# Permuting the stages of an attention step: scores and exponential ahead of transposes and product

## The chip, the cores and the metric

The kernel runs on one core of a Trainium2 chip. The metric is device time in microseconds (us). The kernel before takes 703.48 us (median of 3 runs, 703.40 to 703.51). A core has five engines that matter here, each with a queue that it works off in the order in which the program put the instructions in: TensorE (PE; its weight loads are shown apart as PEld), VectorE (DVE), ScalarE (ACT), GpSimd (POOL) and SyncE (SP, which here issues nearly all DMAs).

## The reference

The first half is an attention in which a query sees only the keys of its own hash bucket; the second is a mixture of four experts, applied to the attention's output.

```python
# q, k, v: (2, 8, 768, 64); proj: (64, 6); batch 2, 8 heads, 768 rows
q_bucket = sum of 2**n * ((q @ proj)[n] > 0);  k_bucket likewise
scores = q @ k.T / 8, and -1e9 where q_bucket != k_bucket
attn = exp(scores - rowmax);  attn /= rowsum + 1e-9
x = (attn @ v), heads side by side: (1536, 512)
p = domain_probs / (rowsum + 1e-9)                 # (1536, 4)
out = sum over e of p[:, e] * (relu(x @ w1[e]) @ w2[e])   # w1 (4, 512, 1024)
```

## The kernel before

The attention goes head by head, 16 heads (`b`, `h`), and each head has six row tiles of 128 rows (`t`). One *step* `i` belongs to tile `i` of all 96. The work of a tile is cut into stages, and stage X of a step handles the tile some steps back (its lag), so that one step holds pieces of several tiles:

- **S** (lines 442 to 463, tile i): four matmuls, two by two, write 128 x 768 negated scores into a PSUM tile `sps` (two of these exist). VectorE copies them to the SBUF tile `p` and takes the row minimum `nb` on the way (line 454).
- **E** (line 470, tile i-1): ScalarE makes the exponential in place, with the row sum as a by-product.
- **T** (lines 502 to 521, tile i-3, the heads of batch 0 only): twice three TensorE transposes into PSUM tiles `ptps` (tag "one", of which there are four, shared with the product `pv` and the hash `hps`). Each triple is copied to SBUF (`pt` or `pth`): the first by ScalarE, the second by VectorE, or by ScalarE too in every third tile (steps 1 and 4 of a head).
- **X** and **Y** (lines 526 to 552, batch 1 only) do the same without TensorE: VectorE transposes 32 x 32 blocks, and two DMAs through DRAM do the rest.
- **V** (lines 554 to 572): the product with `v`, for a whole head. In batch 0 in two halves: the first in step 3 of the next head, one step after the last tile of its own head was transposed, the second in step 5. **U** (lines 577 to 592, step 2 of the head after that) copies the result out, one half by ScalarE, one by VectorE.
- **N**, **R** (lines 475 to 498): reciprocals of the row sums, sent through DRAM and back as a broadcast. **M** (line 594): POOL multiplies by them and splits the result in a high and a low part, every second head.
- **P**: preparation of the next head in four pieces, one per step 0 to 3: high half of q and k on ScalarE (line 376, step 1) and copies of it on POOL (line 265), low half on VectorE (line 379, step 2), hash matmuls (line 391) with the signs of their results on ScalarE (line 401, step 3), then the key columns on POOL (lines 406, 265). P also issues the next loads.

The order of the stages within a step is the string `ORDER`; the program is emitted by hand in this order, and each engine keeps it. For batch 0 the steps run alone, with the first expert's weights split on VectorE and POOL in between. From step 53 on, when the last head of batch 0 has been multiplied out, the MoE starts. Its first half runs over batch 0, and between its groups of matmuls the attention steps of batch 1 are drawn in: S, T and P give back a cost at a `yield`, and as many are drawn as the costs allow. From about 330 us on the MoE is alone.

Of the kernel before, what the change touches and what calls it, by code (L numbers as in the profile page):

```python
# [42 lines left out]
W_SPLIT = 40  # L43
W_STEP = 6
PREP_AT = 0
ORDER = "TXSUVMEYNRP"
LIGHT_FROM = 8
DRAIN = 2000
SPLIT_FIRST = 3
# [7 lines left out]
def tile_lsh_attention__then__domain_moe(  # L57
# [570 lines left out]
    def attention():  # L628
# [76 lines left out]
        for i in range(n + LAG_M[1] + 3):  # L705
            for op in ORDER:
                c = do(op, i)
# [509 lines left out]
```

## Time and profile before

| | |
|---|---|
| Median of 3 runs | 703.48 us |
| The profiled execution | 703.57 us |
| its span, first to last instruction | 701.9 us |
| Busy: TensorE / weight loads | 695.0 / 589.4 us |
| Busy: VectorE / ScalarE / POOL | 515.3 / 330.9 / 307.5 us |
| Granted TensorE clock, mean | 0.999 |

Busy times are sums of instructions. Matmuls overlap each other, so a TensorE that counts as busy may still be waiting; idle time of TensorE is better seen at its weight loads, each of which precedes its matmul. In a timeline a number in brackets is how long the engine was idle before the instruction, and behind the arrow stands what ended last of the things that it waited for; "issue" means that nothing was waited for that the profile shows. In the lists below one line can stand for several equal instructions in a row (x2, x3, x6).

### The profile page before, as it was taken

Reading aid. Unit: us, or ns where it says so; the run is one execution under the profiler, and the core shown is the slowest. Engines: PE = TensorE matmul, PEld = TensorE weight load, DVE = VectorE, ACT = ScalarE, POOL = GpSimd, SP = SyncE. Lnnn points to the kernel's source line nnn. Section 1 sums busy time; section 2 is a strip of 40 time slices with the busy share of each in tenths; the row PEclk is TensorE's granted clock in tenths of the full one; section 3 lists DMA queues with packets and bytes.
Section 4 is the critical chain, followed back from the end, with each engine's and each line's share of the span. In section 5 each row is a group of like instructions: output and inputs, shape, how many; then the busy total and the mean of one; then the engine's idle time right before and its main releaser. Section 6 shows DMA issues by size and latency. Waiting matters only on the chain.

```text
span 701.9 us, 10122 instructions
## 1 busy us (share of the span) xinstructions
PE 695.0 (99%) x3702; PEld 589.4 (84%) x3702; DVE 515.3 (73%) x839; ACT 330.9 (47%) x646; POOL 307.5 (44%) x290
## 2 busy tenths in 40 slices
PE   8999999999999999999999999999999999999998
PEld 7766675878878878877998989899898989989896
DVE  6898898967678568785768786777767667776762
ACT  7887788544543553551424444343333424343330
POOL 6359578623443543461525555342423324232420
PEclk9999999999999999999999999999999999999999
DMA  5323444669979778684221222411123121112202
GB/s 140 67 49 75 88 105 80 233 168 295 253 224 306 219 249 296 215 289 140 60 77 52 83 70 81 149 62 62 62 87 90 50 71 61 61 60 91 81 11 90
DMA packets 83938, 87.77 MB, mean 125 GB/s; under 512 B 52400, under 2 KB 54960, under 8 KB 81840
## 3 DMA queue, kind: packets, MB, share of 16 engines
q1 hardware_dynamic: 82864, 86.79, 41.4%
q8 instruction: 29, 0.48, 0.3%
q10 hardware_dynamic: 1024, 0.33, 0.2%
q14 instruction: 21, 0.17, 0.1%
HBM read 65.04 MB, written 22.07 MB: 124 GB/s over the span
## 4 chain that ended last, share of the span: by engine, by line
PE 94%; DVE 2%; POOL 2%; issue 1%; ACT 1%; DMA 0%; POOLq 0%; DVEq 0%
PE mps L786 13%; PE mps L788 12%; PE mps L787 12%; PE mps L1070 8%; PE mps L1074 8%; PE mps L1073 8%; PE pv L565 8%; PE sps L447 4%; PE sps L449 4%; PE ptps L515 4%; PE mps L836 3%; PE mps L838 3%; PE mps L837 3%; PE hps L391 1%; DVE p L454 1%
## 5 line engine op out<-in xcount | busy, mean ns | idle before, releaser
L786 PE MATMUL mps<-w2hi,hh 128*128 128x512 f32 (+1 forms) x388 | 150.6, 388 | 0.0
L788 PE MATMUL mps<-w2hi,hl 128*128 128x512 f32 (+1 forms) x388 | 150.3, 387 | 0.0
L787 PE MATMUL mps<-w2lo,hh 128*128 128x512 f32 (+1 forms) x388 | 150.3, 387 | 0.0
L1056 POOL TENSOR_TENSOR w2lo<-ws,w2hi 128x512 fp32r<-128x512 f32 x48 | 61.2, 1298 | 148.4 <-ACT w2hi L1055 146.9
L454 DVE TENSOR_SCALAR_CACHE_REDUCE p<-sps 128x768 f32<-128x768 f32 x96 | 90.3, 941 | 27.8 <-PE sps L449 26.1
L470 ACT ACTIVATE p<-p,nb 128x768 f32<-128x768 f32 x96 | 89.5, 932 | 24.1 <-DVE p L454 23.7
L780 DVE SCALAR_TENSOR_TENSOR acc<-mps,pe,acc 128x512 f32<-128x512 f32 (+1 forms) x85 | 63.0, 741 | 45.6 <-PE mps L788 45.2
L1074 PE MATMUL mps<-xo,w1lo 128*128 128x384 f32 x272 | 91.4, 336 | 0.0
L1073 PE MATMUL mps<-xo,w1hi 128*128 128x384 f32 x272 | 91.3, 336 | 0.0
L1070 PE MATMUL mps<-xo,w1hi 128*128 128x384 f32 x272 | 91.3, 336 | 0.0
L1080 ACT ACTIVATE hh<-mps 128x384 fp32r<-128x384 f32 x96 | 47.3, 492 | 92.5 <-PE mps L1074 62.9
L788 PEld LDWEIGHTS mps<-w2hi,hl 128*128 128x128 f32 x388 | 72.9, 188 | 15.2
L786 PEld LDWEIGHTS mps<-w2hi,hh 128*128 128x128 f32 x388 | 72.9, 188 | 14.5 <-issue 0.6
L787 PEld LDWEIGHTS mps<-w2lo,hh 128*128 128x128 f32 x388 | 72.9, 188 | 14.0
L1100 DVE TENSOR_TENSOR mt<-mps,mt 128x384 f32<-128x384 f32 x72 | 40.2, 558 | 45.2 <-PE mps L1074 44.4
L1014 POOL TENSOR_TENSOR w1lo<-ws,w1hi 128x512 fp32r<-128x512 f32 x36 | 49.5, 1378 | 44.3 <-ACT w1hi L1010 17.1
L565 PE MATMUL pv<-pt,tv 128*64 128x384 f32 x288 | 67.1, 492 | 0.0
L1085 DVE SCALAR_TENSOR_TENSOR hl<-mps,hh 128x384 fp32r<-128x384 f32 x96 | 53.4, 556 | 14.7 <-ACT hh L1080 12.4
L1010 ACT ACTIVATE w1hi<-wc 128x512 fp32r<-128x512 f32 x48 | 30.0, 630 | 66.6 <-DVE wc L1019 66.6
L265 POOL TENSOR_SCALAR q<-ah 64x768 fp32r<-64x768 f32 (+1 forms) x33 | 27.1, 822 | 76.2 <-ACT ah L376 61.9
L447 PE MATMUL sps<-ah,q 128*128 128x384 f32 x192 | 54.0, 362 | 0.4 <-DVE p L454 0.4
L534 DVE STREAM_TRANSPOSE t<-p 128x768 f32<-128x768 f32 x48 | 46.2, 964 | 8.5 <-ACT p L470 8.3
(137 smaller groups left out, 1372.2 us busy)
## 6 DMA issues: line engine op xcount, KB each, us to landing
ws<-in_moe_w_dram SPq DMA_DIRECT2D x64, 512.0 KB, 3.8
scr<-t SPq DMA_DIRECT2D x16, 1152.0 KB, 8.0
pt<-scr SPq DMA_DIRECT2D x16, 1152.0 KB, 6.8
tv<-in_v_dram SPq DMA_DIRECT2D x16, 192.0 KB, 5.9
tqk<-in_q_dram SPq DMA_DIRECT2D x30, 96.0 KB, 3.6
out_dram<-acc SPq DMA_DIRECT2D x11, 256.0 KB, 2.0
tqk<-in_k_dram SPq DMA_DIRECT2D x28, 96.0 KB, 3.7
rdb<-row SPq DMA_DIRECT2D x14, 192.0 KB, 4.5
```

What stands on the lines that cost most here:

```text
L447: nc.tensor.matmul(ps[:, i, :NH], q1[:, sl], k1[:, i * NH : (i + 1) * NH], start=True, stop=False)
L454: nc.vector.tensor_scalar(out=two(pt), in0=ps[:, :, :NH], scalar1=MASKED, scalar2=MASKED, op0=ALU.min, op1=ALU.min, accum_out=nb,)
L470: nc.scalar.activation(pt, pt, ACTF.Exp, bias=nb, scale=-1.0, accum_out=dens[b, h, r][:, o : o + 1])
L565: nc.tensor.matmul(dst, vvs[b, h][:, c], pts[b, h, g][c], start=c == 0, stop=c == NT - 1, tile_position=(0, g * D),)
L780: nc.vector.scalar_tensor_tensor(out=acc, in0=ps, scalar=pcol, in1=acc, op0=ALU.mult, op1=ALU.add)
L786: nc.tensor.matmul(ps, hh[:, ts], w2hi[:, f, cs], start=n == 0, stop=False)
L787: nc.tensor.matmul(ps, hh[:, ts], w2lo[:, f, cs], start=False, stop=False)
L788: nc.tensor.matmul(ps, hl[:, ts], w2hi[:, f, cs], start=False, stop=n == FC - 1)
L1056: nc.gpsimd.tensor_tensor(out=lo[:, c + o], in0=t[:, o], in1=hi[:, c + o].bitcast(F32), op=ALU.subtract)
L1070: nc.tensor.matmul(ps, whi[:, kk, fs], xh[kk], start=first and kk == 0, stop=False, skip_group_check=True)
L1073: nc.tensor.matmul(ps, whi[:, kk, fs], xl[kk], start=False, stop=False, skip_group_check=True)
L1074: nc.tensor.matmul(ps, wlo[:, kk, fs], xh[kk], start=False, stop=kk == KH - 1, skip_group_check=True)
```

## The change

The string that gives the order of the stages within a step is permuted: S ahead of T, and E directly behind S. U, V, M, Y, N, R and P keep their places to each other, and so do X and S. Lags, tiles and buffers stay.

```diff
-ORDER = "TXSUVMEYNRP"
+ORDER = "XSETUVMYNRP"
```

## Rows read from the trace of the kernel before

**Rows 1.** The page: the span, and the chain that ended last by engine.

```profile
span 701.9 us, 10122 instructions
...
PE 94%; DVE 2%; POOL 2%; issue 1%; ACT 1%; DMA 0%; POOLq 0%; DVEq 0%
```

**Rows 2.** Waits of weight loads, 125 to 702 us: total us, times, longest.

```profile
PEld sps L447 <- PE pv L565: 3.1, 5, 0.6
```

**Rows 3.** Timeline of weight loads, one head: start us, us, operation [idle <-releaser].

```profile
31.19 0.64 PEld L515 LDWEIGHTS ptps<-ident,p 128*128 128x128 f32 x6 [0.60 <-ACT p L470]
...
33.15 0.30 PEld L447 LDWEIGHTS sps<-ah,q 128*128 128x128 f32 x2
...
33.79 0.76 PEld L515 LDWEIGHTS ptps<-ident,p 128*128 128x128 f32 x6
...
35.15 0.42 PEld L515 LDWEIGHTS ptps<-ident,p 128*128 128x128 f32 x3
35.73 0.31 PEld L515 LDWEIGHTS ptps<-ident,p 128*128 128x128 f32 x3 [0.16 <-DVE pth L519]
...
36.91 0.13 PEld L565 LDWEIGHTS pv<-pt,tv 128*64 128x64 f32 x1 [0.24 <-issue]
...
38.58 0.13 PEld L391 LDWEIGHTS hps<-xt,pf 128*44 128x44 f32 x2 [0.18 <-issue]
...
39.64 0.64 PEld L515 LDWEIGHTS ptps<-ident,p 128*128 128x128 f32 x6 [0.61 <-issue]
...
41.04 0.31 PEld L515 LDWEIGHTS ptps<-ident,p 128*128 128x128 f32 x3
41.55 0.31 PEld L515 LDWEIGHTS ptps<-ident,p 128*128 128x128 f32 x3 [0.21 <-ACT pt L521]
...
42.73 0.13 PEld L565 LDWEIGHTS pv<-pt,tv 128*64 128x64 f32 x1 [0.24 <-issue]
...
44.82 0.64 PEld L515 LDWEIGHTS ptps<-ident,p 128*128 128x128 f32 x6 [0.60 <-ACT p L470]
```

**Rows 4.** Timeline of ScalarE in the same head.

```profile
31.77 0.49 ACT L521 ACTIVATE pth<-ptps 128x384 f32<-128x384 f32 x1 [1.17 <-PE ptps L515]
...
33.12 0.87 ACT L521 ACTIVATE pth<-ptps 128x384 f32<-128x384 f32 x2
33.88 0.94 ACT L470 ACTIVATE p<-p,nb 128x768 f32<-128x768 f32 x1
...
34.80 0.93 ACT L376 ACTIVATE ah<-xt,qk_scale 128x768 fp32r<-128x768 f32 x1
35.63 0.48 ACT L521 ACTIVATE pth<-ptps 128x384 f32<-128x384 f32 x1
36.00 0.48 ACT L592 ACTIVATE xr<-pv 64x384 f32<-64x384 f32 x1
...
39.82 1.17 ACT L401 ACTIVATE k<-hps,sgn_bias 44x384 fp32r<-44x384 f32 x2 [1.13 <-PE hps L391]
41.01 0.87 ACT L521 ACTIVATE pt<-ptps 128x384 f32<-128x384 f32 x2
```

**Rows 5.** Timeline of VectorE in the same head.

```profile
34.24 0.96 DVE L454 TENSOR_SCALAR_CACHE_REDUCE p<-sps 128x768 f32<-128x768 f32 x1 [0.48 <-PE sps L449]
...
36.60 0.56 DVE L590 COPY xr<-pv 64x384 f32<-64x384 f32 x1
...
37.70 1.55 DVE L379 SCALAR_TENSOR_TENSOR al<-xt,qk_scale,ah 128x768 fp32r<-128x768 f32 x1
```

**Rows 6.** Timeline of all engines: a copy, and the product that waited for it.

```profile
119.75 0.47 ACT L521 ACTIVATE pth<-ptps 128x384 f32<-128x384 f32 x1
...
120.36 0.13 PEld L565 LDWEIGHTS pv<-pt,tv 128*64 128x64 f32 x1 [0.26 <-ACT pth L521]
```

**Rows 7.** Timelines of POOL and of weight loads: scores that waited for keys.

```profile
59.15 0.83 POOL L265 TENSOR_SCALAR k<-al 12x768 fp32r<-12x768 f32 x1
...
60.03 0.30 PEld L449 LDWEIGHTS sps<-k,al 76*128 76x128 f32 x2 [0.67 <-POOL k L265]
```

## The prediction

> **What bounds the kernel now.** I read the page first. Of a span of 701.9 us, 94% of the chain that ended last lies on TensorE [rows 1]: to move the time, a change must take idle time away from TensorE or put some in. The second view is what TensorE's weight loads waited for. From 125 us on, where the attention of batch 1 runs between the matmuls of the MoE, no wait is longer than 0.6 us; the largest that isn't the gap inside a product is 3.1 us in 5 pieces, scores behind a product, which is a gap between two kinds of matmul and no wait for data [rows 2]. So only the first 125 us, the attention of batch 0, can react to an order of stages.
>
> There I went through the timelines of three engines for one head (six steps, 31.19 to 44.82 us, 13.63 us). Number a head's steps 0 to 5. TensorE [rows 3] runs transposes, then scores, in each step (1.36 us a step, 33.79 to 35.15); in step 3 also the first half of a product (36.91) and the hash (38.58), in step 5 the second half (42.73). It is a nearly full row: real waits are 0.16 us before the second half of the transposes of step 3 (35.73) and 0.21 us in step 5 (41.55), both for a PSUM buffer that a copy has yet to empty. The 0.60 us before the transposes at 31.19 and 44.82 is put down to an exponential, but it stands before 39.64 too with nothing awaited: it is the gap after a product or a hash. ScalarE [rows 4] has holes: 1.17 us at 31.77, where the copy at its head waits for transposes that stand behind a product, and 1.13 us at 39.82, before the hash's signs.
>
> **The change part by part.** No instruction is added or removed; the string permutes the stages of a step. In batch 1 stage T does nothing and the X, S, V order on TensorE stays, so TensorE's sequence there is the same; only the exponential moves ahead of one copy per head on ScalarE, and one exponential (0.92 us, 33.88 to 34.80) once a head on an engine with holes costs nothing while TensorE has MoE matmuls to stream. If that cover were gone it would be 8 x 0.92 = 7 us; rows 2 show no such wait, so I take 0. The DMAs on SP's queue and POOL's work keep their order; nothing of theirs is moved past anything.
>
> In batch 0 three queues change. TensorE: scores of tile i before the transposes of tile i-3. VectorE: row minimum of i before its copy of i-3. ScalarE: exponential of i-1 before the copies of i-3. The exponential-to-transposes link gets looser. What gets tighter is copies to product: the product's first half in step 3 needs the copy of the tile transposed in step 2, and that copy now stands behind one more exponential, which itself waits for fresh scores.
>
> *Term 1, the product.* Zero is the first instruction after the second half of a product. Before: ScalarE's copy of step 2 starts at 35.63, 4.44 after zero (31.19). A product starts 0.61 after the copy that it waits for began (119.75 to 120.36 [rows 6]), so it could start at 5.05 and starts at 5.72 (36.91): 0.67 to spare. After: the scores come at zero; the minimum begins 1.09 later (33.15 [rows 3] to 34.24 [rows 5]) and lasts 0.96, so the exponential of step 1 begins at 2.05. ScalarE then does, without a hole: exponential 0.92 (2.97), two copies 0.76 (33.12 to 33.88; 3.73), the high half of the next head 0.83 (34.80 to 35.63; 4.56), exponential of step 2 0.92 (5.48), and only now the copy. The product can start at 5.48 + 0.61 = 6.09. TensorE, with the same blocks in swapped pairs, is there at 5.72. It waits 0.37.
>
> *Term 2, the PSUM buffer in step 5.* From product to hash 1.67 (36.91 to 38.58), to the signs 1.24 (38.58 to 39.82), the signs 1.19 (39.82 to 41.01): 6.09 + 4.10 = 10.19. Before, the copies of step 4 follow at once and the transposes go on 0.54 later (41.01 to 41.55). After, the exponential comes first: copy at 11.11, transposes at 11.65. TensorE wants them at 6.09 + 2.73 (36.91 to 39.64) + 1.36 + 0.64 (33.15 to 33.79) + 0.31 (the first half, 41.04) = 11.13. It waits 0.52 where it waited 0.21.
>
> A rule of the Trainium skill would have term 2 otherwise: Perfetto Trace Analysis, Optimization Strategy, says that the same gap repeating on an engine that should be full can mean too few buffers for the next tile. The wait of 0.21 for a PSUM buffer repeats so [rows 3]. It is a rival below.
>
> *The head.* From the second half of the transposes of step 5 to the product 42.73 - 41.55 = 1.18, less the scores (0.64) that now stand earlier: 0.54; then 2.09 to the next zero (42.73 to 44.82): 11.65 + 0.54 + 2.09 = 14.28, against 13.63. That is +0.65 a head, for six whole heads +3.9 us.
>
> *Ends of the stretch.* In the first head with a product there is no product before it in whose shadow ScalarE could run ahead; its copy has one exponential more in front: +0.92, and +0.31 of term 2, together 1.2. After the last head of batch 0 the same pattern stands once more before the MoE begins, with the signs in front of the exponentials: I take a head's worth, 0.7 (0 if the work there hides it, 1.3 if two exponentials and not one are late).
>
> *POOL.* VectorE's half of the product's copy-out starts 0.60 after ScalarE's (36.00 to 36.60), the low half 1.10 later [rows 4, 5]. Before: 6.51 after zero. After: 5.48 + 0.37 + 0.60 + 1.10 = 7.55. POOL makes the next head's keys from it, 1.04 later, while the scores that need them come 14.28 - 13.63 - 0.60 = 0.05 later than before (the old ones stand behind 0.60 of transposes). Once that copy was already the last to end, by 0.67 us [rows 7]; that wait grows by 1.0. Two other heads have the same POOL work: 0 to 1.0 each, I take 0.3 for both, as their scores did not wait before.
>
> Sum: 3.9 + 1.2 + 0.7 + 1.3 = 7.1 us, on the profiled execution's own 703.57 us (span 701.9 and 1.7 around it), which is 0.09 above the median of 703.48. Forecast: 710.6 us. Bounds of the terms: the head from +0.4 (term 2 as before, or a release faster by 0.1 to 0.2) to +0.9; ends 0.9 to 2.5; POOL 0 to 3: from 703.57 + 3.3 = 706.9 to 703.57 + 10.9 = 714.5.
>
> **The rivals.**
> *A, faster.* The decisive link is exponential to transposes: now an exponential has a further half step, ScalarE fills its 1.17 us hole with work ready, and TensorE loses its waits: six heads by 0.37 and the 0.67 of rows 7 make 2.9 us, 700.7. For it: the 0.60 labels and the hole. Against: those labels stand where nothing is awaited, and in the new order ScalarE's hole returns, as the first exponential of a head needs scores that also stand behind the product. It decides if the copy of step 2 starts less than 5.11 after zero.
> *B, no change.* TensorE streams either way and the waits only change names: 703.5. For it: 94%. Against: term 1 turns a reserve of 0.67 into -0.37, and no work stands behind the product that could pass it.
> *C, buffers and not order.* The wait in step 5 stays at 0.21, because it belongs to the number of PSUM buffers, which is kept. Seven times 0.31 less: 708.4. The rule named above would give this. Against: the copy that empties the buffer does move behind an exponential.
> *D, VectorE as the new late one, slower still.* The minimum of step 3 stands behind the low half: 7.55 + 1.55 [rows 5] = 9.10, exponential possible at 10.06, and ScalarE wants it at 10.19. With 0.13 to spare, any cast of a weight in front puts it 0.4 to 0.8 later; in all seven heads by 0.7 that is 4.9 more: 715.5. Against: only eight casts lie in the stretch.
>
> **How the numbers follow.** Forecast 0.57 (own range 706.9 to 714.5), A 0.09, B 0.07, C 0.15, D 0.12. Two tenths of a per cent, 1.4 us, is what a measurement can tell from no change. Faster is A, 0.09; same is B, 0.07; slower the rest, 0.84. The range leaves A and B out (0.16) and little of D: 705.0 to 716.0.
>
> **What would show it.** In the profile after: heads of about 14.3 us between first product halves instead of 13.63; before the first half of most products an idle of TensorE of 0.3 to 0.5 us put down to ScalarE's copy; before the second half of step 5's transposes one of some 0.5; ScalarE's hole at a head's start now in front of an exponential, with VectorE's minimum as releaser; scores waiting for POOL's key copy longer than 0.67 once or more; nothing new after some 133 us. Wrong it is if heads keep 13.6 us or less, if product halves start without a wait for the copy, or if the difference shows in the MoE.

## The result and the profile after

The kernel after takes 711.68 us (median of 4 runs, 711.08 to 712.12); the kernel before, run beside it, takes 703.5 (703.4 to 703.58). The ratio is 1.0115, with a 95% interval of 1.0099 to 1.0131: slower, by 8.2 us. The forecast was 710.6.

The page of the profiled execution (712.12 us) answers to [rows 1]. TensorE's share of the chain that ended last falls from 94% to 86%, and ScalarE's rises from 1% to 6%. TensorE, VectorE, ScalarE and POOL ran as many instructions as before (9179 together); the 12 fewer in the total are of kinds that are not counted as busy.

```profile
span 710.4 us, 10110 instructions
...
PE 86%; ACT 6%; DVE 3%; POOL 2%; DMA 1%; issue 1%; ACTq 0%; POOLq 0%; DVEq 0%
```

Where the 8.5 us of span lie is read from marks on TensorE's weight loads: the first instruction after the second half of a product ("zero"; seven of them bound the six whole heads), and the first matmul of the MoE (line 836).

| stretch | before | after | more | predicted |
|---|---|---|---|---|
| start to first zero | 31.19 | 33.47 | 2.28 | 1.2 |
| six heads | 82.69 | 87.64 | 4.95 | 3.9 + 1.3 (POOL) |
| last zero to first MoE matmul | 11.56 | 12.20 | 0.64 | 0.7 |
| from there to the end | | | 0.63 | 0 |

The six heads took 13.63, 13.63, 14.26, 13.99, 13.62 and 13.56 us before, and take 14.29, 15.08, 14.95, 14.28, 14.75 and 14.29 after. Three of them have the forecast length, three are longer.

The timeline of weight loads answers to [rows 3]; the rows up to 47.76 are one head (14.29 us), 58.91 and 63.52 lie in and behind a long one (63.52 answers to [rows 7]), and 138.67 is in the MoE.

```profile
33.47 0.30 PEld L447 LDWEIGHTS sps<-ah,q 128*128 128x128 f32 x2 [0.60 <-issue]
...
39.50 0.13 PEld L565 LDWEIGHTS pv<-pt,tv 128*64 128x64 f32 x1 [0.41 <-ACT pth L521]
...
43.62 0.31 PEld L515 LDWEIGHTS ptps<-ident,p 128*128 128x128 f32 x3 [0.33 <-ACT k L401]
...
45.19 0.31 PEld L515 LDWEIGHTS ptps<-ident,p 128*128 128x128 f32 x3 [0.23 <-ACT pt L521]
...
47.76 0.30 PEld L447 LDWEIGHTS sps<-ah,q 128*128 128x128 f32 x2 [0.60 <-POOL w1lo L745]
...
58.91 0.31 PEld L515 LDWEIGHTS ptps<-ident,p 128*128 128x128 f32 x3 [1.33 <-DVE pt L519]
...
63.52 0.30 PEld L449 LDWEIGHTS sps<-k,al 76*128 76x128 f32 x2 [0.38 <-POOL k L265]
...
138.67 0.19 PEld L837 LDWEIGHTS mps<-xs,w1hi 128*128 128x128 f32 x1 [0.67 <-POOL xs L608]
```

The product's first half (39.50) now waits for ScalarE's copy; before, it waited for no data [rows 3]. The list of waits from 5 to 137 us (total us, times, longest) gives that wait 3.7 us, and as much to VectorE's copy of step 3:

```profile
PEld ptps L515 <- DVE pt L519: 3.7, 5, 1.3
PEld pv L565 <- ACT pth L521: 3.7, 8, 0.8
```

ScalarE in the same head answers to [rows 4] and shows why the product waits. The exponential of step 1 starts when its minimum is done, 2.07 after zero; behind it stand two copies, the high half and one more exponential, and only then, 5.50 after zero, comes the copy that releases the product, with no hole in between.

```profile
34.81 0.49 ACT L521 ACTIVATE pth<-ptps 128x384 f32<-128x384 f32 x1 [1.37 <-PE ptps L515]
35.54 0.94 ACT L470 ACTIVATE p<-p,nb 128x768 f32<-128x768 f32 x1 [0.24 <-DVE p L454]
...
36.48 0.85 ACT L521 ACTIVATE pth<-ptps 128x384 f32<-128x384 f32 x2
37.22 0.93 ACT L376 ACTIVATE ah<-xt,qk_scale 128x768 fp32r<-128x768 f32 x1
38.05 0.93 ACT L470 ACTIVATE p<-p,nb 128x768 f32<-128x768 f32 x1
...
38.97 0.48 ACT L521 ACTIVATE pth<-ptps 128x384 f32<-128x384 f32 x1
```

VectorE in the long head (47.76 to 62.84) answers to [rows 5]. The low half (line 379) takes 2.00 us, the minimum stands behind it, and the copy at 58.30 behind the minimum; that copy is what the transposes at 58.91 waited 1.33 us for.

```profile
54.27 0.56 DVE L590 COPY xr<-pv 64x384 f32<-64x384 f32 x1 [0.64 <-ACT xr L592]
...
55.40 2.00 DVE L379 SCALAR_TENSOR_TENSOR al<-xt,qk_scale,ah 128x768 fp32r<-128x768 f32 x1
57.42 0.96 DVE L454 TENSOR_SCALAR_CACHE_REDUCE p<-sps 128x768 f32<-128x768 f32 x1
...
58.30 0.55 DVE L519 COPY pt<-ptps 128x384 f32<-128x384 f32 x1
```

ScalarE at the change to the MoE: the last copy-out of batch 0 (135.19) stands behind an exponential that waited for its minimum, and POOL's scaled operands, made from it, come late for the matmuls at 138.67.

```profile
134.13 0.94 ACT L470 ACTIVATE p<-p,nb 128x768 f32<-128x768 f32 x1 [0.72 <-DVE p L454]
...
135.19 0.48 ACT L592 ACTIVATE xr<-pv 64x384 f32<-64x384 f32 x1
```

### The profile page after: what moved, and what is told of

Same layout as the page of the kernel before. It is cut to its first block, busy times and chain, and to the rows that moved or that the text cites. A ratio compares the mean times of both kernels' runs of the same rounds, so it can differ in the third digit from the quotient of the medians.

```text
span 710.4 us, 10110 instructions
## 1 busy us (share of the span) xinstructions
PE 698.9 (98%) x3702; PEld 592.7 (83%) x3702; DVE 508.9 (72%) x839; ACT 330.7 (47%) x646; POOL 308.6 (43%) x290
## 4 chain that ended last, share of the span: by engine, by line
PE 86%; ACT 6%; DVE 3%; POOL 2%; DMA 1%; issue 1%; ACTq 0%; POOLq 0%; DVEq 0%
PE mps L786 12%; PE mps L788 12%; PE mps L787 12%; PE mps L1070 8%; PE mps L1074 8%; PE mps L1073 8%; PE pv L565 8%; PE sps L447 3%; PE mps L837 3%; PE mps L838 3%; PE mps L836 3%; PE sps L449 3%; ACT p L470 3%; DVE p L454 1%; ACT pth L521 1%
```

## The experiments

Each was timed beside the kernel before (medians 703.42 to 703.57 there); the one without weight splits is a single run. Theory: with the exponential ahead, ScalarE's copies stand behind an exponential that waits for fresh scores, and the copies release TensorE. Rivals: scores first is itself the cost (TensorE's order, buffers emptied late); VectorE's minimum or POOL's keys are the late ones.

| kernel | us | ratio [95%] | six heads, us |
|---|---|---|---|
| scores first only | 707.99 | 1.0065 [1.0050, 1.0081] | 14.83 14.32 14.99 14.27 14.16 14.26 |
| exponential first only | 724.76 | 1.0303 [1.0289, 1.0317] | 18.19 18.18 15.62 15.63 16.64 15.62 |
| exponential right behind scores | 706.67 | 1.0047 [1.0034, 1.0060] | 13.87 14.79 14.00 13.89 13.94 13.67 |
| after, weights split at the end | 722.69 (one) | | 14.29 14.28 14.29 14.29 14.28 14.29 |
| after, high half a step later | 711.29 | 1.0111 [1.0096, 1.0126] | 14.04 13.95 15.51 13.94 15.88 13.94 |
| after, copies first in step 4 | 709.22 | 1.0084 [1.0067, 1.0101] | 14.06 15.07 14.95 13.96 14.15 13.98 |
| after, both of these | 710.31 | 1.0098 [1.0083, 1.0113] | 13.83 13.79 15.13 13.76 16.02 13.77 |
| scores first, high half later | 711.46 | 1.0114 [1.0099, 1.0129] | 13.91 14.42 15.73 14.42 16.00 14.42 |
| after, VectorE's copy of step 3 on ScalarE | 711.10 | 1.0108 [1.0095, 1.0122] | 14.28 14.89 14.87 14.29 14.29 14.28 |
| that, and copies first in step 4 | 708.67 | 1.0074 [1.0058, 1.0089] | 13.76 14.33 14.87 13.76 14.29 13.76 |
| before, VectorE's copy of step 3 on ScalarE | 703.49 | 0.9998 [0.9989, 1.0007] | |
| before, exponential first in step 0 | 703.51 | 1.0001 [0.9992, 1.0010] | |

**Which of the two moves costs.**

```diff
-ORDER = "XSETUVMYNRP"
+ORDER = "XSTUVMEYNRP"   # scores first only
+ORDER = "ETXSUVMYNRP"   # exponential first only: ahead of the transposes, scores behind them
+ORDER = "TXSEUVMYNRP"   # exponential right behind the scores, transposes ahead as before
```

*Scores first only.*

> Scores ahead of the transposes, the exponential where it was before (order XSTUVMEYNRP). Theory (the copies standing behind the exponential cost the time): the product's copy starts at 5.1 after the head's zero, the product waits for nothing, heads of 13.4 to 13.7 us, 702.0 to 704.5 us in all. Rival (scores first costs the time, because VectorE's minimum of a tile now stands ahead of its copy and empties a PSUM buffer late): heads stay at 14.0 us or more, 706.5 to 710 us.

Measured: 707.99. The theory's number was missed and the rival's met: scores first costs 4.6 us without the exponential. Products no longer wait for a copy, as the theory had it, but transposes do. In the head with zero at 89.06 ScalarE's copy of step 2 starts 5.40 after zero, and the transposes of step 3 wait 0.60 for it:

```profile
90.59 0.49 ACT L521 ACTIVATE pth<-ptps 128x384 f32<-128x384 f32 x1 [2.03 <-PE ptps L515]
...
94.46 0.48 ACT L521 ACTIVATE pth<-ptps 128x384 f32<-128x384 f32 x1
...
94.99 0.31 PEld L515 LDWEIGHTS ptps<-ident,p 128*128 128x128 f32 x3 [0.60 <-ACT pth L521]
```

The list of waits shows two more late ones beside it, VectorE's copies and POOL's keys:

```profile
PEld ptps L515 <- DVE pt L519: 2.7, 5, 0.9
PEld ptps L515 <- ACT pth L521: 2.6, 5, 0.6
PEld sps L449 <- POOL k L265: 2.4, 4, 1.3
```

*Exponential first only.*

> The exponential ahead of the copies, transposes still ahead of scores (order ETXSUVMYNRP). Theory: ScalarE's first exponential of a head can start only 2.65 after zero (scores at 0.60, minimum 1.09 later, 0.96 long), the product's copy at 6.1 and the product at 6.7, second transposes of step 5 at 12.2: heads of 15.0 to 15.6 us, 713 to 718 us. Rival (scores first costs the time): heads as before, 13.6 us, 703 to 705 us.

Measured: 724.76, above what was expected. A clean head is 15.62, the longest in any of these kernels. In the head with zero at 85.43 the exponential starts 2.67 after zero, and two triples of transposes wait over 1 us for ScalarE's copies behind an exponential; the copy of step 2 starts 6.09 after zero:

```profile
88.10 0.94 ACT L470 ACTIVATE p<-p,nb 128x768 f32<-128x768 f32 x1 [1.59 <-DVE p L454]
...
89.55 0.31 PEld L515 LDWEIGHTS ptps<-ident,p 128*128 128x128 f32 x3 [1.10 <-ACT pth L521]
...
91.52 0.48 ACT L521 ACTIVATE pth<-ptps 128x384 f32<-128x384 f32 x1
...
97.79 0.31 PEld L515 LDWEIGHTS ptps<-ident,p 128*128 128x128 f32 x3 [1.25 <-ACT pt L521]
```

The heads of 18.2 us have more behind them. The second of them (51.63 to 69.81) and the head of 16.64 (101.06 to 117.70) have the same two waits in steps 4 and 5, one for VectorE's copy and one for ScalarE's:

```profile
62.51 0.31 PEld L515 LDWEIGHTS ptps<-ident,p 128*128 128x128 f32 x3 [1.17 <-DVE pt L519]
...
65.02 0.50 PEld L515 LDWEIGHTS ptps<-ident,p 128*128 128x128 f32 x3 [1.18 <-ACT pt L521]
...
111.92 0.31 PEld L515 LDWEIGHTS ptps<-ident,p 128*128 128x128 f32 x3 [1.17 <-DVE pt L519]
...
114.44 0.31 PEld L515 LDWEIGHTS ptps<-ident,p 128*128 128x128 f32 x3 [1.17 <-ACT pt L521]
```

The windows behind the second wait follow. Columns: us, then busy us of TensorE, weight loads, VectorE, ScalarE and POOL; granted clock; DMA share; GB/s.

```profile
66.00:68.00 2.00, 2.00 (x8) 1.16 (x9) 1.28 (x2) 0.64 (x3) 1.77 (x3) 0.50 0.04 8
...
114.00:116.00 2.00, 1.56 (x11) 1.14 (x13) 1.01 (x4) 2.00 (x5) 1.47 (x2) 1.00 0.75 272
116.00:118.00 2.00, 2.00 (x15) 0.86 (x12) 1.92 (x5) 1.09 (x3) 0.00 (x0) 1.00 0.04 1
```

In the first of the two heads the granted clock falls to 0.50, the 1.2 GHz level; in the other it stays at 1.00. Why it falls in one and not in the other is not shown. Of the 2.6 us that this long head has above a clean one, about 1.0 comes with the wait for VectorE's copy (16.64 - 15.62) and 1.5 with the clock (18.18 - 16.64).

So the moves don't add up: +21.3 us alone (some 3 of them with the low clock, if both long heads lose 1.5 to it), +4.6 alone, +8.2 together. In the kernel after, the same exponential starts 2.07 after zero (35.54 - 33.47): with the scores first its minimum comes 0.60 earlier, and part of what exponential first costs is taken back.

*Exponential right behind the scores.*

> Old order, but the exponential directly behind the scores and so ahead of U, V and M (TXSEUVMYNRP): it passes the copy-out of the product on ScalarE, in both batches, and not the copies of the transposes. Theory: heads within 0.1 us of before, and at the change to the MoE a wait of 0.5 to 0.7 us of TensorE for the last operand that POOL makes, because the copy-out stands behind one more exponential: 703.5 to 704.3 us. Rival (an exponential moved ahead costs wherever it passes a copy, batch 1 included): 0.4 us per head in 14 heads, 708 us or more.

Measured: 706.67, between the two expectations. The attention of batch 1 is free, as the theory had it (no new wait behind 150 us). In batch 0 the theory's "within 0.1 us" failed: the six heads are 1.5 us longer together, and 1.2 of it is one head (14.79 against 13.63). There VectorE's half of the copy-out U starts 6.39 after zero instead of 5.78, since it stands behind ScalarE's half and that behind the exponential; the low half and VectorE's copy follow it, and the copy starts at 9.56 instead of 8.17. At the change to the MoE POOL's operands are late:

```profile
132.12 0.19 PEld L836 LDWEIGHTS mps<-xs,w1hi 128*128 128x128 f32 x1 [0.86 <-POOL xs L605]
...
133.20 0.19 PEld L837 LDWEIGHTS mps<-xs,w1hi 128*128 128x128 f32 x1 [0.90 <-POOL xs L608]
```

That is 1.76 us there, of the same kind as the 0.67 of the kernel after.

**Where the three long heads come from.**

```diff
-W_STEP = 6
+W_STEP = 1000
```

Weights are no longer split between the heads, but all in one piece ahead of the MoE; nothing is left out.

> The changed kernel, with the splitting of the first expert's weights (casts on VectorE, differences on POOL) taken out of the steps of batch 0 and left for the end of them in one piece. Theory: the three longer heads (15.08, 14.95 and 14.75 us) have VectorE late by these casts and by a slower low half beside POOL's differences: all six heads then take 14.2 to 14.5 us; the whole is longer, as the weights come in one piece before the MoE. Rival (VectorE is late by the order alone): the three heads keep 14.7 us or more.

All six heads are 14.28 or 14.29 long, and the low half takes 0.98 to 0.99 us in every one. So the long heads come from the weight splits on VectorE and POOL (the run moves both and does not tell them apart), and 14.28 is what the order alone makes. The whole is slower (722.69): the MoE waits 3.0 us for the split of its weights on POOL, and 5.0 us for operands that POOL scales behind that split. The weight loads of one of these heads, zero to zero:

```profile
60.80 0.30 PEld L447 LDWEIGHTS sps<-ah,q 128*128 128x128 f32 x2 [0.60 <-issue]
...
66.83 0.13 PEld L565 LDWEIGHTS pv<-pt,tv 128*64 128x64 f32 x1 [0.41 <-ACT pth L521]
...
72.53 0.31 PEld L515 LDWEIGHTS ptps<-ident,p 128*128 128x128 f32 x3 [0.30 <-ACT pt L521]
...
75.09 0.30 PEld L447 LDWEIGHTS sps<-ah,q 128*128 128x128 f32 x2 [0.60 <-issue]
```

**The two waits of the forecast, taken away one at a time.** The first edit moves the high half (line 376) out of the way of the copy that the product needs; the second gives ScalarE the copies ahead of the exponential in step 4 alone, which concerns the wait in step 5.

```diff
-            steps.setdefault(SPLIT_AT[late], []).append("hi")
+            steps.setdefault(SPLIT_AT[late] + (not late), []).append("hi")
...
-            for op in ORDER:
+            for op in "XSTEUVMYNRP" if i % NT == 4 and i < H * NT else ORDER:
```

> The changed kernel with one ScalarE operation of 0.83 us (the high half of the next head, batch 0) moved from the end of step 1 to the end of step 2, so behind the copy that the product waits for. Theory (the product waits because ScalarE's chain from the first scores of a head to that copy is too long): the copy starts at 4.65 after zero instead of 5.48, the first half of the product no longer waits, the wait for a PSUM buffer in step 5 stays: heads without weight casts 13.9 us instead of 14.28, in all 708 to 710 us. Rival (the wait has another cause, such as VectorE's half of the copies or the PSUM buffers): heads stay at 14.28, 711 us or more.

Clean heads go from 14.28 to 13.94, as expected: with zero at 45.51 the copy starts 4.69 after zero, and the product no longer waits for it.

```profile
50.20 0.47 ACT L521 ACTIVATE pth<-ptps 128x384 f32<-128x384 f32 x1
...
51.20 0.13 PEld L565 LDWEIGHTS pv<-pt,tv 128*64 128x64 f32 x1 [0.17 <-DVE w1hi L755]
```

The total (711.29) missed, for the later high half makes POOL's keys late in four scores, by 5.4 us together.

> The changed kernel, but in step 4 of each head of batch 0 the transposes and their copies stand ahead of the exponential again. Theory: the second transposes of step 5 no longer wait for that exponential; what is late next is VectorE's copy of step 3, so only 0.25 to 0.5 us of a head is won: heads without casts 13.8 to 14.05 us, in all 708.5 to 710.5 us; the product goes on waiting 0.4. Rival (the wait belongs to the number of buffers): 14.28 as before, 711 to 712 us.

Clean heads 13.96 to 14.06, as expected, and 709.22.

> Both edits together in the changed kernel. Theory: the two waits of ScalarE's making are gone, heads without casts 13.4 to 13.7 us, about as before the change, in all 705 to 707.5 us. Rival (VectorE's minimum ahead of its copy is a bound of its own): 13.9 us or more, 708 us or more.

Clean heads 13.76 to 13.83, just above the 13.4 to 13.7 expected and the 13.63 before. The two edits nearly add: 0.34 and 0.2 to 0.3 alone, 0.45 to 0.52 together. What is left in most of these heads is a wait of 0.38 for VectorE's copy. The total (710.31) lies in the rival's range; POOL's keys are late again (5.9 us in 4 waits).

**Scores first with the high half later.**

```diff
-ORDER = "XSETUVMYNRP"
+ORDER = "XSTUVMEYNRP"
...
-            steps.setdefault(SPLIT_AT[late], []).append("hi")
+            steps.setdefault(SPLIT_AT[late] + (not late), []).append("hi")
```

> Scores ahead of the transposes, exponential where it was before, and the high half of the next head moved to the end of step 2. Theory: in the kernel with scores first alone the second transposes of step 3 waited 0.6 us for a PSUM buffer that ScalarE's copy of step 2 (5.16 to 5.4 after zero) empties; that copy now starts at 4.3, the wait goes, heads without casts 13.4 to 13.7 us, in all 702 to 705 us, no slower than 1.5 us above the kernel before. Rival (scores first costs by VectorE): heads 14 us or more, 707 us or more.

Measured: 711.46; the theory's 702 to 705 fell, and the rival's range was met. ScalarE's copy is no longer waited for, and VectorE's takes its place: the low half waits for the high half and pushes minimum and copy back. POOL's keys are late as well (5.7 us in 4 waits). Both come with the later high half, so this run does not show what scores first alone costs by VectorE.

```profile
112.44 1.62 DVE L379 SCALAR_TENSOR_TENSOR al<-xt,qk_scale,ah 128x768 fp32r<-128x768 f32 x1 [0.98 <-ACT ah L376]
114.09 0.96 DVE L454 TENSOR_SCALAR_CACHE_REDUCE p<-sps 128x768 f32<-128x768 f32 x1
...
114.97 0.55 DVE L519 COPY pt<-ptps 128x384 f32<-128x384 f32 x1
115.58 0.31 PEld L515 LDWEIGHTS ptps<-ident,p 128*128 128x128 f32 x3 [1.06 <-DVE pt L519]
```

**VectorE's copy of step 3 given to ScalarE.** That step transposes a head's tile 0, so the edit exempts tile 0 from VectorE.

```diff
-            if i and o % 2 == 0:
+            if i and o % 2 == 0 and t:
```

> The changed kernel with only the second copy of a head's first tile (step 3) on ScalarE instead of VectorE. Theory: the waits for VectorE's copy in step 4 (0.24 to 1.33 us) go, ScalarE has room for it beside the product; heads that were 14.28 stay there, as ScalarE bounds them, and 15.08, 14.95 and 14.75 fall to 14.3 to 14.6 us; in all 709 to 710.5 us. Rival (VectorE's copy only fills time in which another engine is late anyway): nothing changes, 711 to 712 us.

One long head shrinks to the clean length (14.75 to 14.29), the other two stay near 14.9: in the first ScalarE's exponential waits 0.62 for the same late minimum, in the second 0.19, and scores at its start wait 0.48 for POOL's keys. The theory's 709 to 710.5 was missed; the total (711.10) can't be told from that of the kernel after.

> The changed kernel with transposes and copies ahead of the exponential in step 4 (as in the run before), and with the second copy of a head's first tile (step 3) on ScalarE instead of VectorE. Theory (the order has two costs: copies behind an exponential on ScalarE, and VectorE's copy of step 3 behind a minimum that stands behind the low half): only the product's 0.4 is left, heads of 13.7 to 13.9 us, the three long heads too (but for a wait for POOL's keys), in all 706 to 708 us. Rival (the long heads and the rest come from POOL or from the buffers): 14.0 us and long heads as before, 709 us or more.

With the copies first in step 4 as well, clean heads are 13.76, as expected. The other three are not: in one (14.33) scores wait 0.54 for VectorE's minimum, in two (14.87 and 14.29) 1.03 and 0.58 for POOL's keys. The total is 0.7 above what was expected.

**Is there anything to gain in the kernel before?** The same edit of the copy there, and the exponential first in a head's step 0 only, where ScalarE has its hole:

```diff
-            for op in ORDER:
+            for op in "ETXSUVMYNRP" if i % NT == 0 and i < H * NT else ORDER:
```

> The kernel before with the same copy on ScalarE. Theory: in the old order this copy stands ahead of the minimum and nobody waits for it; 0.47 us less on VectorE in a head takes away at most the one wait of 0.5 us behind a weight cast: 702.9 to 703.6 us. Rival (VectorE bounds the old order too): 702 us or less.

> The kernel before, but in step 0 of each head of batch 0 the exponential stands ahead of the transposes' copies, where ScalarE had a hole of 1.17 us behind the product. Theory: the hole was free time, the copies come up to 0.9 us earlier and nobody waits for them: 703.2 to 703.8 us. Rival (ScalarE's hole costs TensorE time, the reason for which the new order could have been faster): 0.3 us a head, 701.5 us or less.

703.49 and 703.51, both no change, as expected. In the second the copies do not come earlier, though: with zero at 44.78 the copy of step 2 starts 4.45 after it, against 4.44 [rows 4], since ScalarE now waits for the next transposes.

```profile
49.23 0.48 ACT L521 ACTIVATE pth<-ptps 128x384 f32<-128x384 f32 x1
```

So an exponential put into ScalarE's hole of 1.17 us gains nothing. No version tried here beats the kernel before.

## Why the prediction was right, and where it was off

**Where the kernel can react: right but for 0.63 us.** From 140 us on the largest wait that isn't the gap inside a product is the one of [rows 2], with the same 3.1 us in 5 pieces. The eight exponentials of batch 1 cost nothing. What failed is "nothing new after some 133 us": the copy-out U of the last head of batch 0 is one of the things that the exponential is moved past, and the sum had no term for it (the 0.67 at 138.67). The run with the exponential right behind the scores shows the same wait at 1.76.

**Term 1, the product: right.** The exponential was put at 2.05, the copy at 5.48 and the product at 6.09 after zero, with a wait of 0.37; they start at 2.07, 5.50 and 6.03 (39.50 - 33.47). The 0.41 of idle time there holds a gap of 0.17 that stays when the copy is early (51.20 with the high half later). That run has the product at 5.69, and its clean heads are 0.34 shorter: this is what the wait costs.

**Term 2, step 5: right in sum, one wait in two places.** Forecast: second half of the transposes at 11.65 after zero, waiting 0.52. Measured: 11.72 (45.19 - 33.47), with 0.23 there and 0.33 at 43.62 behind the signs, 0.56 together. The sign named in the forecast, some 0.5 in step 5, did not come: the wait there is about the 0.21 of before. The run with copies first in step 4 takes 0.2 to 0.3 of it back.

**The head: right.** 14.28 forecast; 14.28 to 14.29 in three heads and in all six where the weight splits are out of the way.

**Two other signs came otherwise.** ScalarE's hole at a head's start is still in front of a copy (34.81, 1.37 us); only 0.24 of waiting stands in front of the exponential. And in the six heads scores waited at most 0.38 for POOL's keys, not over 0.67.

**Ends.** The one before the MoE was right (0.64 against 0.7). The first head was not: 2.28 against 1.2. Part of the difference is TensorE's clock, which no step had:

```profile
8.00:10.00 2.00, 1.38 (x7) 1.12 (x7) 0.82 (x2) 1.74 (x3) 1.70 (x4) 1.00 0.95 133
10.00:12.00 2.00, 1.66 (x8) 1.04 (x7) 1.97 (x5) 1.29 (x3) 1.86 (x3) 0.96 0.79 203
12.00:14.00 2.00, 2.00 (x9) 1.91 (x9) 2.00 (x5) 1.02 (x3) 0.91 (x2) 0.50 0.89 316
14.00:16.00 2.00, 2.00 (x11) 1.93 (x10) 1.04 (x3) 1.24 (x4) 0.26 (x1) 0.68 0.02 4
```

In these windows of the kernel after, the granted clock is at the 1.2 GHz level (0.50) from 12 to 14 us and 0.68 on average in the next two, where before it was 1.00; from 8 to 12 us TensorE is busy for 3.04 us (1.38 + 1.66), before for 3.55. Of the four runs the two with a mean clock of 0.998 took 712.0 and 712.12, the two with 1.000 took 711.08 and 711.37: about 0.8 us, if the clock is all that differs. The other 0.3 is not accounted for.

**The POOL term: wrong in place, and right in size by luck.** The keys were to cost 1.3 us more. They cost 0.38 once instead of 0.67; it was VectorE that was late, and the six heads take 4.95, which is 0.65 x 6 = 3.9 and 1.05. That is rival D in three heads of six, where the low half took 1.55 to 2.00 us (0.98 in the other three; the forecast had 1.55 in all) and the copy behind the next minimum was late by 0.88 to 1.33. D's price of 0.7 a head was about right for the heads that have it (0.80, 0.67 and 0.47 above 14.28); in exchange the waits that made two heads longer before (14.26 and 13.99) are gone, which is why 1.9 more in three heads is 1.05 net.

**The total.** The span grew by 8.5 us where the sum had 7.1: the first head adds 1.08 to it and the time from the first MoE matmul on 0.63, while the six heads are 0.25 and the end before the MoE 0.06 below.

**The rivals.** A needed ScalarE's hole to matter; the exponential filled into it alone changes nothing (703.51), and the copy starts 5.50 after zero, past A's limit of 5.11. B fell by the interval. C read the repeating gap as a lack of PSUM buffers, after the rule of the Trainium skill (Perfetto Trace Analysis, Optimization Strategy). The trace agrees on the wait in step 5 itself, which stays (0.23 against 0.21), but not on the head: with the buffers as they were, order alone made it 14.28, 13.96 or 13.76. No run changed the number of buffers, so what more of them would give is not shown.

**What the sum did not say.** Both moves have a price, not only the exponential's. Behind each product ScalarE waits once more, and from there to the copy of step 2 it works without a hole. Where that last wait ends sets the copy (us after zero):

| order | last wait is ahead of | ends at | work up to the copy | copy of step 2 | clean head |
|---|---|---|---|---|---|
| before | copy of step 0 | 0.58 | 3.86 | 4.44 | 13.6 |
| scores first only | copy of step 0 | 1.53 | 3.87 | 5.40 | 14.2 to 14.3 |
| after | exponential of step 1 | 2.07 | 3.43 | 5.50 | 14.28 |
| exponential first only | exponential of step 1 | 2.67 | 3.42 | 6.09 | 15.62 |

Scores first alone puts the transposes, and so the copy of step 0, behind the scores; the exponential then stands behind that copy and is late with it. The copy's time orders the heads; it doesn't give their lengths, since different things wait: transposes of step 3 for this copy in the second row, the product for it in the third, and in the fourth transposes of step 2 for the copies ahead of it (89.55). Not settled: which copy a triple of transposes waits for differs between these kernels though the buffers are asked for in one order, and why the clock falls at the start in some executions only, or in some heads.

## What to carry to other kernels

Where a queue is worked off in order, price a permutation by the copies that others wait for: what stands ahead of each one, and does that wait for something fresh? A move of a stage counts for every instruction that it passes, the ones at the seam between two phases too, and two moves are priced together, as one can undo what the other costs. Find the head that nothing else disturbs (here by moving the weight splits away) before fitting a model to a mean of heads.

## What the runs showed of the hardware that was not expected

- VectorE's low half, with two inputs in SBUF, takes 0.98 to 0.99 us where no POOL instruction runs beside it (all six heads without weight splits, three of six after the change) and 1.42 to 2.00 where one does (the other three, and all six before the change); the 2.00 at 55.40 ran beside POOL's `w1lo` (next row). The Trainium skill (SBUF — State Buffer, Who interferes with whom) says that such an instruction contends with a POOL instruction that reads SBUF; the trace agrees, with 1.02 us added where POOL's instruction runs on for 1.18 us from 55.40.

```profile
55.31 1.27 POOL L745 TENSOR_TENSOR w1lo<-ws,w1hi 128x512 fp32r<-128x512 f32 x1
```

- The same waits of TensorE can cost different amounts: with exponential first alone a head with waits of 1.17 and 1.18 us for copies took 18.18 us, with the clock at 0.50 behind them, and one with waits of 1.17 and 1.17 took 16.64 with the clock at 1.00. What separates the two is not shown.
- Before the change a hole of 1.17 us on ScalarE, once a head, was worth nothing: the exponential put into it left the time at 1.0001 [0.9992, 1.0010], and the copies behind it came no earlier.
